# The second gate of an adaLN block held as four columns until the feed-forward, the "+1" of the scale columns moved into the accumulation, and a new order of the work

## The chip, the cores and the metric

The kernel runs on one core of one Trainium2 chip. The metric is the device time of one execution in microseconds (us). Before the change the median of three runs is 200.48 us (200.16 to 200.75). The profiled execution took 200.58 us; its trace spans 198.8 us from the first instruction to the last, and all positions in time below are counted from the start of that span.

## The reference

The block is an adaLN-conditioned transformer layer: a linear attention with learned feature maps, then a gated feed-forward, each behind a layer norm with a scale and a shift that come from a conditioning vector `c`, and each added back through a gate that comes from `c` too.

```python
mod = (_silu(c) @ w_mod).reshape(c.shape[0], 6, 1, -1)
sa, ca, ga, sb, cb, gb = ...                     # six rows of 512
h = _layernorm(x) * (1 + ca) + sa
x = x + ga * _A_ref(h, wqkv, w_phi, wo)          # phi_q, phi_k: softmaxes over 16, twice; linear attention; @ wo
h = _layernorm(x) * (1 + cb) + sb
x = x + gb * _B_ref(h, w_gate, w_up, w_down)     # silu(h @ w_gate) * (h @ w_up) @ w_down
```

`x` is 2048 x 512 in bfloat16, there are 32 heads of 16, and the feed-forward is 1376 wide.

## The kernel before, in words

**Tiles and stages.** The 2048 tokens are 16 tiles of 128, in four chunks of 512. The program runs in three stages that overlap.

The first stage loads `x`, the weights and `w_mod`, forms silu(c) as columns (`silucT`), and folds the feature map into the query and key weights (`fold_phi`, lines 518 to 533). `mod_cols` (lines 463 to 481) forms eight columns of the modulation at a time: 32 TensorE matmuls (line 471) with 128x128 pieces of `w_mod` as weights and one column of `silucT` as data leave four shift columns and four scale columns in one PSUM bank. VectorE copies the shifts (line 476) and copies the scales with 1.0 added (line 477) into `modA` for the first norm and `modB` for the second. `first_norm` and `turn_tile` normalize the first tiles, turn them on TensorE (line 561) and write them, scaled and shifted, as `hT` (ScalarE line 568, VectorE line 570); later tiles are turned by a transposing DMA (`raw`, line 582) and scaled by VectorE, ScalarE or GpSimd (lines 591 to 594).

The second stage takes each tile through `k_tile` (keys on line 625, exponentials on ScalarE line 636, sums on VectorE line 643, values on line 629, products on GpSimd lines 657 to 669), `kv_tile` (accumulation over all tiles into the PSUM tile `kv_ps`, line 675) and `q_tile` (queries line 698, exponentials line 702, sums line 706, the product on GpSimd line 713, and a transposing DMA to `pT`, line 717). `gate(0)` and `gate(1)` (lines 724 to 733) form the two gates here, already spread over all 128 partitions: four 512-column matmuls each, with one column of `silucT` broadcast to 128 as weights (line 730), and a ScalarE copy into `gab` (line 733). GpSimd multiplies the first gate into the output projection (`wo_sb`, line 774).

The third stage takes each tile through `attend` (line 821 on TensorE, lines 824 and 828 on VectorE), a turn, `project` (line 862, then the residual add on line 865 and the statistics of the second norm), the second norm (`xn`, GpSimd line 398 for the first tiles), its turn (`modulate_T`, TensorE line 414, written with `modB` by lines 422 and 425), and the feed-forward (gate and up matmuls on line 920, the narrow last block on line 965, silu on 927, the product on 930 or 936, down matmuls on line 997). The second gate `gab[:, 1]` enters at the very end of a tile, where VectorE multiplies the down result by it (line 1008), and in `wdg` (line 946), half of the down weights with the gate multiplied in, for half of the last tile.

**What sets the order.** Every piece of work is recorded as an operation with its possible engines. A list of numbers, `ORDER` (lines 47 to 87), says in which order they are placed and which alternative each takes (a number's quotient by four is the operation, its remainder the alternative); the class `Plan` places them in that order with assumed durations. Each engine then executes its own operations strictly in the order written, and the SyncE queue issues the DMAs in its own. Six PSUM banks (`one_ps`) are handed out by the same plan. Where the plan expects TensorE to be idle it inserts matmuls of ones on line 1064 (`fill`) whose result is thrown away; there are 26 of them.

## Time and profile before

| | TensorE | VectorE | ScalarE | GpSimd |
|---|---|---|---|---|
| busy, us of 198.8 | 193.6 | 136.2 | 114.1 | 126.5 |

| group of instructions | times | busy, us | mean of one, ns |
|---|---|---|---|
| line 730, a gate: matmul of 512 columns | 8 | 2.1 | 378 |
| line 471, modulation: matmul of 1 column | 64 | 2.0 | 163 |
| line 733, gate copy on ScalarE, 128x512 | 2 | 1.2 | 598 |
| line 774, gate into `wo_sb` on GpSimd, 128x512 | 4 | 4.5 | 1152 |
| line 946, gate into `wdg` on GpSimd, 128x1024 | 2 | 4.2 | 2124 |
| line 713, query product on GpSimd, 128x512 | 16 | 16.8 | 1055 |
| line 476, line 477: copies of four columns on VectorE | 2 and 2 | 0.3 and 0.3 | 157 and 152 |

The duration of one matmul is from its start to its modelled end, and neighbours overlap. What a row of them costs is read from the distance of their starts: four of 512 columns take 0.86 us in the chain of waits, sixteen of one column 0.38 to 0.41 us. In the same way one GpSimd product of 128x512 follows the next after 1.01 to 1.05 us. A busy share near 100% on TensorE counts the filling matmuls too.

### The profile page before, as it was taken

What the parts mean: (1) busy time and instruction counts of PE and PEld (TensorE: products, weight loads), DVE (VectorE), ACT (ScalarE), POOL (GpSimd) and SP (SyncE); (2) the same over time, 40 slices, a digit from 0 to 9 for tenths busy, and PEclk for the clock granted to TensorE, in tenths of its full rate; (3) what the DMA queues carried; (4) which work ended last, traced back from release to release, by engine and by line L of the source; (5) the groups of instructions that cost most, each with busy time, mean ns of one, the idle gap of its engine ahead of it and who ended that gap; (6) DMA issues with size and microseconds to landing.
All of it is one profiled execution on the core that took longest, in us unless ns stands there. A gap on an engine that the chain in (4) does not pass through costs nothing.

```text
span 198.8 us, 4150 instructions
## 1 busy us (share of the span) xinstructions
PE 193.6 (97%) x1529; PEld 115.6 (58%) x1529; DVE 136.2 (69%) x274; ACT 114.1 (57%) x247; POOL 126.5 (64%) x196
## 2 busy tenths in 40 slices
PE   7999999999999999999999999999999999999993
PEld 2755555554565788689766768667444444444442
DVE  5898999999998999999999588452420214340233
ACT  2699999999979975416556544624026510255300
POOL 3377999999999477958956676266725320042841
PEclk9999999999999999999999999999999999999999
DMA  6998997799632883689895543201030000020012
GB/s 210 340 325 191 271 236 239 172 408 244 174 68 53 154 105 74 116 155 148 164 134 104 107 96 66 53 26 43 0 119 0 0 5 26 0 79 0 31 57 76
DMA packets 50983, 24.18 MB, mean 122 GB/s; under 512 B 42161, under 2 KB 47762, under 8 KB 50962
## 3 DMA queue, kind: packets, MB, share of 16 engines
q1 hardware_dynamic: 50816, 23.85, 50.7%
q8 instruction: 12, 0.20, 0.4%
q14 instruction: 9, 0.07, 0.1%
q10 hardware_dynamic: 146, 0.07, 0.1%
HBM read 11.58 MB, written 2.10 MB: 69 GB/s over the span
## 4 chain that ended last, share of the span: by engine, by line
PE 87%; POOL 5%; ACT 4%; DMA 2%; DVE 1%; issue 1%; POOLq 0%; DVEq 0%
PE one_ps L920 35%; PE one_ps L997 19%; PE one_ps L629 7%; PE one_ps L862 6%; PE one_ps L625 5%; PE one_ps L698 3%; PE kv_ps L1064 3%; PE one_ps L965 3%; POOL wo_sb L774 2%; ACT hT L568 2%; PE kv_ps L821 2%; DMA pT<-eq 2%; PE kv_ps L675 2%; ACT e L636 1%; POOL eq L713 1%; PE one_ps L730 1%
## 5 line engine op out<-in xcount | busy, mean ns | idle before, releaser
L920 PE MATMUL one_ps<-hT,wgu_sb 128*128 128x256 bf16 (+2 forms) x560 | 74.7, 288 | 0.0
L920 PEld LDWEIGHTS <-wgu_sb 128*128 128x128 bf16 x560 | 48.3, 98 | 24.0
L927 ACT ACTIVATE sg<-one_ps 128x512 bf16<-128x512 f32 (+1 forms) x41 | 23.7, 587 | 40.4 <-PE one_ps L920 38.9
L936 POOL TENSOR_TENSOR gu<-usb,sg 128x512 bf16<-128x512 bf16 x18 | 20.7, 1153 | 31.4 <-ACT sg L927 25.7
L997 PE MATMUL one_ps<-wd_sb,gu 128*128 128x512 bf16 (+2 forms) x176 | 39.6, 372 | 0.0
L930 DVE TENSOR_TENSOR gu<-one_ps,sg 128x512 bf16<-128x512 f32 (+1 forms) x23 | 15.2, 659 | 29.5 <-PE one_ps L920 22.4
L997 PEld LDWEIGHTS <-gu 128*128 128x128 bf16 (+1 forms) x187 | 18.1, 98 | 18.0
L1008 DVE TENSOR_TENSOR fg<-one_ps,gab 128x512 bf16<-128x512 f32 (+1 forms) x16 | 10.7, 668 | 21.0 <-PE one_ps L997 21.0
L348 DVE BATCH_NORM_STATS2 st<-x_c 128x6 f32<-128x512 bf16 x32 | 21.2, 678 | 0.2
L643 DVE TENSOR_REDUCE S<-e 128x64 f32<-128x1024 bf16 x16 | 19.0, 1200 | 0.4 <-ACT e L636 0.2
L706 DVE TENSOR_REDUCE Sq<-eq 128x64 f32<-128x1024 bf16 x16 | 19.0, 1195 | 0.0
L934 ACT CAST usb<-one_ps 128x512 bf16<-128x512 f32 x18 | 10.5, 586 | 12.9 <-PE one_ps L920 12.8
L702 ACT ACTIVATE eq<-one_ps 128x512 bf16<-128x512 f32 x32 | 17.1, 609 | 0.1
L713 POOL TENSOR_TENSOR eq<-eq,Rq 128x512 bf16<-128x512 bf16 x16 | 16.8, 1055 | 0.5
L636 ACT ACTIVATE e<-one_ps 128x512 bf16<-128x512 f32 x32 | 16.8, 618 | 0.0
L1012 POOL TENSOR_TENSOR ot<-x_c,fg 128x512 bf16<-128x512 bf16 (+1 forms) x10 | 11.0, 1105 | 8.1 <-DMA out_dram<-ot 4.3
L862 PE MATMUL one_ps<-wo_sb,oT 128*128 128x512 bf16 x64 | 15.9, 379 | 0.0
L629 PE MATMUL one_ps<-wv,hT 128*128 128x512 bf16 x64 | 15.6, 379 | 0.2 <-ACT e L636 0.2
L698 PE MATMUL one_ps<-wq,hT 128*128 128x512 bf16 x64 | 15.8, 379 | 0.0
L625 PE MATMUL one_ps<-wk,hT 128*128 128x512 bf16 x64 | 15.7, 379 | 0.0
L398 POOL TENSOR_SCALAR xn<-x_c,ln_mv,ln_nmr 128x512 bf16<-128x512 bf16 x14 | 10.6, 768 | 1.8 <-DVE ln_nmr L384 1.8
L669 POOL TENSOR_TENSOR e<-e,S 128x512 bf16<-128x512 bf16 x11 | 11.5, 1054 | 0.1
(118 smaller groups left out, 276.6 us busy)
## 6 DMA issues: line engine op xcount, KB each, us to landing
wmod_sb<-in_w_mod_dram SPq DMA_DIRECT2D x2, 1024.0 KB, 6.5
out_dram<-ot SPq DMA_DIRECT2D x15, 128.0 KB, 1.9
x_c<-in_A_x_dram SPq DMA_DIRECT2D x3, 512.0 KB, 4.4
wgu_sb<-in_B_w_gate_dram SPq DMA_DIRECT2D x1, 1376.0 KB, 6.4
wgu_sb<-in_B_w_up_dram SPq DMA_DIRECT2D x1, 1376.0 KB, 10.3
wd_sb<-in_B_w_down_dram SPq DMA_DIRECT2D x1, 1280.0 KB, 6.3
wmod_sb<-in_w_mod_dram SPq DMA_DIRECT2D x2, 512.0 KB, 6.1
wk<-in_A_wqkv_dram SPq DMA_DIRECT2D x1, 512.0 KB, 4.8
```

The lines of the kernel that those rows point to most:

```text
L348: pl.op("DVE", r=reads, w=[st6], us=0.6, fn=lambda: nc.vector.bn_stats(st6()[:], src))
L625: nc.tensor.matmul(pk()[:], lhsT=hT[c_i][k][:, cols], rhs=Wk2[:, k, :], start=(k == 0), stop=(k == KD - 1))
L629: nc.tensor.matmul(v()[:], lhsT=hT[c_i][k][:, cols], rhs=wv_sb[:, k, :], start=(k == 0), stop=(k == KD - 1))
L636: nc.scalar.activation(e()[:, :, sg].rearrange("p g h f -> p g (h f)"), pk()[:].rearrange("p (g n) -> p g n", g=G), ACT.Exp, scale=(1.0, - ...
L643: pl.op("DVE", r=[e], w=[Ss], us=1.14, fn=lambda: nc.vector.tensor_reduce(Ss()[:].rearrange("p g s h -> p (g s h)"), e()[:].rearrange("p g ...
L698: nc.tensor.matmul(pq()[:], lhsT=hT[c_i][k][:, cols], rhs=Wq2[:, k, :], start=(k == 0), stop=(k == KD - 1))
L706: pl.op("DVE", r=be, w=[Sq], us=1.14, fn=lambda: nc.vector.tensor_reduce(Sq()[:].rearrange("p g s h -> p (g s h)"), eq[:].rearrange("p g s ...
L862: nc.tensor.matmul(a()[:], lhsT=oT()[:, j0 + j, :], rhs=wo_sb[:, j, :], start=(j == 0), stop=(j == KD - 1))
L920: nc.tensor.matmul(ps_()[0:fsz, q * n:(q + 1) * n], lhsT=wgu_sb[:, k, i, m * P:m * P + fsz], rhs=h2[k], start=(k == 0), stop=(k == KD - 1))
L927: pl.op("ACT", r=[g, btab], w=[sg], us=0.08 + 0.41 * L / CW, fn=lambda: nc.scalar.activation(sg()[0:fsz, 0:L], g()[0:fsz, 0:L], ACT.Silu))
L936: pl.op("POOL", r=[usb, sg], w=[gu], us=0.17 + 0.98 * L / CW, fn=lambda: nc.gpsimd.tensor_tensor(gu()[0:fsz, 0:L], usb()[0:fsz, 0:L], sg() ...
L997: nc.tensor.matmul(fp()[:], lhsT=b()[0:fsz, c0:c0 + P], rhs=wd_[0:fsz, m, wcs], start=(m == 0), stop=(m == FM - 1))
```

## The change

The change has four parts.

1. **Second gate as columns.** `gate(1)` no longer makes 512-column matmuls. Sixteen one-column matmuls (line 751 of the changed file) leave the gate as four columns of 128 in PSUM, and one small copy (line 754, on VectorE) puts them in `gcol`. The first gate stays as it was.
2. **Spread later.** A new `spread_gate`, recorded just before the feed-forward's weights are prepared, writes a matrix with four 128x128 blocks, each the identity times one column of the gate (line 761, recorded for GpSimd or VectorE; the order takes GpSimd), sums it over the partitions with one 512-column matmul whose weights are all ones (line 765), and copies the result to `gab[:, 1]` (line 766, on ScalarE). The end of the preparation now waits for `gcol` in place of the spread gate.
3. **The 1 of the scales in PSUM.** In `mod_cols` one more matmul (line 480: a row of ones against four ones) adds 1 to the four scale columns in the bank, so that one copy of eight columns takes the place of a copy and an add, and may be on VectorE (as for `modA`) or on ScalarE (as for `modB`). The option of reading the scales straight from PSUM for the first tiles is written in but switched off (`early = False`).
4. **A new `ORDER`.** The whole list is different, so the order of instructions on every engine, the order of the DMAs, the engines chosen and the filling matmuls differ too.

Read from the two built programs, with a number for each that the prediction uses: the filling matmuls go from 26 to 24 (two of them in the third stage before, one after). The two halves of the first `w_mod` load had followed each other; now a 256 KB piece of `x` is queued between them. Of the two later 1 MB loads of `w_mod` the one with the second gate comes first. The columns of `modB` are now formed about 2.7 us of matmuls earlier in the TensorE order. All statistics of the third chunk (line 348) now stand before the first key sum on VectorE. Line 761 stands on GpSimd behind the four `wo_sb` products and one query product, and ahead of two query products and the second norm of tile 0; a `wdg` product of 128x512 stands between the second norms of tiles 0 and 1. The two large loads of the gate and up weights (`wgu_sb`) now stand behind two `pT` transposes and the down weights in the DMA queue.

```diff
 ORDER = [
-    0, 4, 44, 8, 48, 64, 52, 12, 16, 68, 76, ...
+    0, 4, 8, 44, 12, 132, 48, 20, 136, 116, 64, ...
...
                 nc.tensor.matmul(mp()[:, n:n + 1], lhsT=wmod_sb[:, k, (n0 + n) * P:(n0 + n + 1) * P],
-                                 rhs=silucT[:, k:k + 1], start=(k == 0 and n == 0), stop=(k == KD - 1),
+                                 rhs=silucT[:, k:k + 1], start=(k == 0 and n == 0), stop=(k == KD - 1 and n < KD),
                                  skip_group_check=True)
+            if k == KD - 1:
+                nc.tensor.matmul(mp()[:, KD:2 * KD], lhsT=ones[0:1, 0:P], rhs=ones[0:1, 0:KD], start=False, stop=True,
+                                 skip_group_check=True)
 
         def fc():
-            nc.vector.tensor_copy(mt[:, 0:KD], mp()[:, 0:KD])
-            nc.vector.tensor_scalar_add(mt[:, KD:2 * KD], mp()[:, KD:2 * KD], 1.0)
+            nc.vector.tensor_copy(mt[:], mp()[:])
...
-        pl.op("DVE", r=[mp], w=[b], us=0.2, fn=fc)
+        pl.op([("DVE", 0.1, fc), ("ACT", 0.2, lambda: nc.scalar.copy(mt[:], mp()[:]))], r=[mp], w=[b])
...
     def gate(gi):
         col0 = (2 * D, 5 * D)[gi]
+        if gi == 0:
...
+            return
+        mp = bank("fold", [P, KD])
+
+        def fm():
+            for k in range(KD):
+                for j in range(KD):
+                    nc.tensor.matmul(mp()[:, j:j + 1], lhsT=wmod_sb[:, k, col0 + j * P:col0 + (j + 1) * P], rhs=silucT[:, k:k + 1],
+                                     start=(k == 0 and j == 0), stop=(k == KD - 1), skip_group_check=True)
+        pl.op("PE", r=[bsil, bm2[gi]], w=[mp], us=0.43, fn=fm)
+        pl.op([("DVE", 0.1, lambda: nc.vector.tensor_copy(gcol[:], mp()[:])),
+               ("ACT", 0.2, lambda: nc.scalar.copy(gcol[:], mp()[:]))], r=[mp], w=[bgcol])
+
+    def spread_gate():
+        bd = Buf()
+
+        def fd(eng):
+            eng.tensor_tensor(gab[:, 1].rearrange("p (j m) -> p j m", j=KD), ident_b[:].unsqueeze(1).to_broadcast([P, KD, P]),
+                              gcol[:].unsqueeze(2).to_broadcast([P, KD, P]), op=ALU.mult)
+        pl.op([("POOL", 1.02, lambda: fd(nc.gpsimd)), ("DVE*", 0.62, lambda: fd(nc.vector))], r=[bgcol], w=[bd])
         t = bank("fold")
...
+        pl.op("PE", r=[bd], w=[t], us=0.216, fn=lambda: nc.tensor.matmul(t()[:], lhsT=ones[:, 0:P], rhs=gab[:, 1], start=True, stop=True))
+        pl.op([("ACT", 0.49, lambda: nc.scalar.copy(gab[:, 1], t()[:])), ("DVE", 0.6, lambda: nc.vector.tensor_copy(gab[:, 1], t()[:]))],
+              r=[t, bd], w=[bgab[1]])
...
-    turned = pl.op("NONE", r=bKVZ + bgab + [bmodB, bmodA] + bWq2, w=[bturn], us=0.0, fn=f_turn)
+    turned = pl.op("NONE", r=bKVZ + [bgab[0], bgcol] + [bmodB, bmodA] + bWq2, w=[bturn], us=0.0, fn=f_turn)
...
+    spread_gate()
     wdg = wts.tile([P, FM, D // 2], BF16, name="wdg")
```

## The prediction

> **What bounds the kernel now.** I read four views in this order: the engine totals, busy time by stage, the chain of waits, and the timelines of TensorE and GpSimd around the place where the chain leaves TensorE. First the busy times of TensorE, its weight loads, VectorE, ScalarE and GpSimd in three stages (clock, DMA share and GB/s at the end of a row):
>
> ```profile
> 20.00:40.00 20.00, 20.00 (x171) 10.55 (x169) 19.41 (x32) 19.84 (x47) 20.00 (x29) 1.00 0.90 232
> 40.00:57.00 17.00, 17.00 (x148) 9.09 (x147) 16.58 (x22) 16.27 (x44) 16.92 (x22) 1.00 0.84 254
> 57.00:68.00 11.00, 10.93 (x105) 6.30 (x104) 10.39 (x26) 9.60 (x24) 8.83 (x14) 1.00 0.36 69
> ```
>
> From 20 to 57 us four engines are full at once, so a saving on one of them alone moves nothing by itself. After 68 us only TensorE is full. The chain that ended last says who leads (start, length, what):
>
> ```profile
> 53.77 0.88 PE one_ps L629 x4
> 54.65 0.26 POOL S L661
> 54.91 0.07 issue
> 54.98 1.06 POOL e L669
> 56.03 3.33 POOL wo_sb L774 x3
> 59.36 0.21 POOL Rq L709
> 59.57 1.11 POOL wo_sb L774
> 60.69 1.01 POOL eq L713
> ...
> 64.41 3.22 DMA pT<-eq
> ...
> 67.68 0.43 PE kv_ps L821 x8
> ```
>
> For ten microseconds the chain is GpSimd, then one transposing DMA; before and after it is TensorE. The two timelines show how close they run (GpSimd's norm of tile 0, then TensorE's turn of it):
>
> ```profile
> 64.37 0.77 POOL L398 TENSOR_SCALAR xn<-x_c,ln_mv,ln_nmr 128x512 bf16<-128x512 bf16 x1
> ```
>
> ```profile
> 65.08 0.42 PE L821 MATMUL kv_ps<-KVZ,pT 128*128 128x68 bf16 x8
> 65.33 0.39 PE L414 MATMUL one_ps<-ident_b,xn 128*128 128x128 bf16 x4
> 65.56 1.03 PE L698 MATMUL one_ps<-wq,hT 128*128 128x512 bf16 x4
> ```
>
> The norm ends at 65.14 and the turn starts at 65.33 without idle time: GpSimd and TensorE meet there with no slack on either side. I call that start T0. Counting matmul columns at 0.2166 us per 512 in the two orders, exactly 127.5 us of matmuls stand behind T0 in both kernels. So the change in time is the shift of T0, plus the waits that TensorE gains or loses behind it. Behind T0 the trace of before has two, 0.15 us in the first gate matmuls and 0.22 us ahead of the fifth attend tile (67.68, waiting for the `pT` of the chain). From there to 194.2 us TensorE runs without a wait.
>
> **What the skill says.** The Trainium skill, "Perfetto Trace Analysis", section Optimization Strategy: a kernel can have several regimes with different most-contended engines, and one looks in the regime for what blocks. The rows above agree: full on four engines, then TensorE alone. "TensorE: Matmul & The Clock Gate", section Back-to-back issue gap, gives about 25 ns as the floor for up to 64 columns and 518 cycles at 2.4 GHz, 216 ns, for 512; the trace has 0.38 to 0.41 us for sixteen one-column matmuls of line 471 and 0.86 us for the four of line 730, so both prices hold here. "DMA: Bandwidth & Descriptors", section Why a DMA increments its semaphore by 16 and not by 1: a transfer counts as landed when the last of its engines is done. The trace agrees: the second 1 MB piece of `w_mod`, issued at 25.91 us, had all but one or two of its packets started by 31 us and landed at 33.10.
>
> **The change, part by part.**
>
> *Second gate.* TensorE loses 0.86 us (line 730) before the attention and gets sixteen one-column matmuls there, 0.40 us (as line 471): -0.46. Later it gets one 512-column matmul, 0.22 us, where a filling one of the same size is dropped, so behind the last key-value product nothing changes. ScalarE's copy of 0.60 us moves from the full stage to about 62 us, where a query exponential waits behind it; the small copy of `gcol`, 0.15 us as on line 476, goes to VectorE. The spread itself is not in the trace. Its nearest row is line 713, a GpSimd product of the same 128x512 with a broadcast operand: 1.055 us each, 1.02 as distance. Bounds are 1.0 and 1.15 (line 774, no broadcast). I take 1.02. It stands on GpSimd behind the four `wo_sb` products and one query product; behind it are two query products, and then the norm that T0 waits for. So it is paid in full on the chain shown above: +1.02.
>
> *The 1 in PSUM.* Two tiny matmuls, 0.05 us on TensorE. A copy and an add of 0.15 us each, overlapping, become one copy: some 0.1 us of VectorE, not on the chain. I cost it at nothing.
>
> *Filling matmuls.* 4.79 us of columns become 4.47. They fill time that TensorE spends waiting anyway: nothing.
>
> *The new order, start.* The second half of the first `w_mod` load now follows 256 KB of `x`. In the trace these landings are 9.37 us for the half and 10.04 for the next 256 KB, so it lands 0.67 later, and `modA` is ready near 11.0 instead of 10.23. ScalarE began writing `hT` at 10.73; now it also has one more pair of lines 377 and 378 first, 0.47 us, so 11.2. Four of line 568 at 0.345 us later the first keys can start: 12.7 instead of 12.18. But ScalarE writes ten of these, not twelve: its key exponentials start at 11.2 + 3.45 = 14.65, before 14.85.
>
> *GpSimd to T0.* In before its first key product (line 661) is at 18.95, and it is then busy without a gap over 0.1 us until `wo_sb` at 55.99: 37.04 us. In after this stretch has no statistics pair (lines 381 and 382, -1.34), one norm less (-0.75), one small copy less (-0.17), one `hT` piece more (+0.52) and one line 709 more (+0.21): 35.5 us. It starts later: VectorE has all the statistics of the third chunk first, so its first sum runs 16.95 to 18.1; ScalarE's reciprocal comes after seven exponentials and copies, 14.65 + 4.22 + 0.47 = 19.35; GpSimd's product starts near 19.7. So `wo_sb` starts at 19.7 + 35.5 = 55.2, 0.8 earlier. From there to the norm before took 64.37 - 55.99 = 8.38; now 8.38 - 0.21 + 1.02 = 9.19. The norm runs 64.4 to 65.15, and T0 by GpSimd is 65.15 + 0.19 = 65.35.
>
> *TensorE to T0.* The last key-value product started at 55.34 and ended at 56.37. Now +0.5 for the late start, -0.46 for the gate, -0.33 for filling between the first keys, -0.3 of a 0.4 us wait at 17.6 us that the other order of values should shed: 54.75. One wait is new. `modB`'s 32 matmuls, at 33.67 in before just behind the landing at 33.10, are now reached at 30.8, and all keys, values and queries are queued behind them. The load is issued behind two transposes that I put 1.4 us earlier, so with the same 7.2 us it lands at 31.65; it may be sooner, since the 512 KB of `wo_sb` no longer follow directly. Wait between 0 and 0.85; I take 0.35. Then 55.1, end 56.0, and T0 by TensorE is 65.33 - 0.4 = 64.95. It waits 0.4 us there for GpSimd. The matmul of ones on line 765 waits for the spread too, done at 55.2 + 4.45 + 1.05 + 1.02 = 61.7; TensorE gets there at 61.8, and behind it are only the projection of tile 1 and queries.
>
> *Behind T0.* The fifth attend tile is reached 1.3 us later in the order, so its `pT` has landed: -0.22. The 128x512 `wdg` product, 1.1 us as half of line 946, stands ahead of the norm of tile 1: done by 69.6, needed at 69.9, so hidden. The weights of line 920 arrive about 57 us, needed at 66. The tail, 194.2 us to the end, has the same last operations.
>
> *Sum.* +0.02 at T0, -0.22 behind it: -0.2, so 200.48 - 0.2 = 200.3.
>
> **The rivals.** *Faster, GpSimd is early.* If GpSimd's stretch before `wo_sb` shrinks by more than worked out, TensorE sets T0. Without the `modB` wait it ends the products at 55.6 and reaches T0 at 64.6: -0.73 - 0.22, 199.5. For it: TensorE had next to no wait in this stage, and every key tile is placed earlier (the last by 1.8 us of matmuls). Against it: GpSimd's 37 us without a gap.
>
> *Slower, `modB` waits.* If the second-gate-first order of the loads brings the other piece where it landed before, 33.10, TensorE stands 2.3 us: products end at 58.0, T0 67.0, +1.65 - 0.22, 201.9. If it lands halfway, at 32.4, the wait is 1.6 and T0 66.3: 201.2. A GpSimd stretch with 0.5 us of gaps adds as much, since the norms of tiles 0 and 1 then both come late. I put this case at 201.3. For it: that landing lagged its packets by 2 us. Against it: the issue is earlier and less is queued behind.
>
> **How the numbers follow.** The meeting at T0 with GpSimd last: 0.44, 200.3. TensorE last: 0.32, 199.5. A new wait: 0.24, 201.3. The range 199.3 to 201.4 leaves out about 0.1 on each side. The spread's bounds (1.0 to 1.15) move the middle case by 0.1. Faster by over 0.3% means below 199.9: nine tenths of the second case and a sixth of the first, 0.36. Slower means above 201.1: most of the third, 0.24. Between: 0.40.
>
> **What would show it.** The chain of waits of after should go through GpSimd lines 761 and 722 into the turn on line 415, with 0.2 to 0.6 us of TensorE idle there; the `wo_sb` products should start near 55.2; the first keys near 12.7; the wait of `modB` under 0.9. No GpSimd wait at T0 means the second case. Over 1 us idle at line 476, or idle at the turn of tile 1, means the third. A new TensorE wait after 75 us would be a cause that I have not seen.

## The result, and the profile after

The changed kernel took 201.57 us (median of six runs, 201.28 to 201.94) against 200.66 us (200.16 to 201.14) for the kernel before on the same chip: a ratio of 1.0048, 95% interval 1.0029 to 1.0066. It is slower by about 0.9 us, and lies 0.17 us above the range that I gave. The ratios here and below leave out single runs that lie more than 1.5% above the fastest of the same kernel; the medians do not. Run again later, instruction for instruction the same, it gave 201.68 us and 1.0031 (1.0011 to 1.0051). The profiled execution took 201.28 us, the shortest of the six; its trace spans 199.5 us, 0.7 more than before.

Busy time by stage, the three windows of the prediction, for the changed kernel (TensorE, its weight loads, VectorE, ScalarE, GpSimd; clock, DMA share and GB/s at the end):

```profile
20.00:40.00 20.00, 19.70 (x181) 10.40 (x179) 20.00 (x30) 19.38 (x49) 20.00 (x28) 1.00 0.71 180
40.00:57.00 17.00, 17.00 (x149) 9.09 (x147) 15.84 (x22) 15.82 (x45) 16.58 (x24) 1.00 0.94 295
57.00:68.00 11.00, 10.88 (x98) 6.08 (x96) 10.22 (x26) 9.78 (x23) 9.65 (x13) 1.00 0.32 64
```

VectorE and GpSimd are less busy than before in the second window (15.84 us against 16.58, and 16.58 against 16.92), and still the third stage starts later. In the first window TensorE is idle for 0.30 us; before it was not. The chain of waits around the same place as in the prediction (start, length, what):

```profile
54.73 0.26 POOL S L670
55.06 1.06 POOL e L678
56.12 0.21 POOL Rq L718
56.34 4.46 POOL wo_sb L808 x4
60.79 1.01 POOL eq L722
61.80 1.01 POOL gab L761
62.85 0.38 PE one_ps L765
...
66.07 0.38 PE one_ps L415 x4
```

The spread (line 761) stands in the chain as forecast, 1.01 us long, but the chain leaves GpSimd at line 765, the matmul of ones, not at the norm of tile 0. The `wo_sb` products start at 56.3, not at 55.2. TensorE's timeline, and GpSimd's norm of tile 0:

```profile
30.39 1.03 PE L707 MATMUL one_ps<-wq,hT 128*128 128x512 bf16 x4
31.64 0.95 PE L476 MATMUL one_ps<-silucT,wmod_sb 128*128 128x1 bf16 x32 [0.23 <-DMA wmod_sb<-in_w_mod_dram]
32.52 0.17 PE L480 MATMUL one_ps<-ones 1*128 1x4 bf16 x1
32.63 0.43 PE L684 MATMUL kv_ps<-va,e 128*128 128x68 bf16 x8
...
62.85 0.38 PE L765 MATMUL one_ps<-gab,ones 128*128 128x512 bf16 x1
...
66.06 0.40 PE L415 MATMUL one_ps<-ident_b,xn 128*128 128x128 bf16 x4
```

```profile
65.22 0.78 POOL L399 TENSOR_SCALAR xn<-x_c,ln_mv,ln_nmr 128x512 bf16<-128x512 bf16 x1
```

The start of tile 0's turn, T0, is at 66.06 in place of 65.33: +0.73. The last matmul starts at 195.86 in place of 195.10: +0.76. So behind T0 nothing is gained or lost in sum, and nearly all of the difference is made before T0. Of the 0.73, 0.38 is a later start (first keys at 12.56 in place of 12.18), and 0.43 lies between the first `wo_sb` product and T0 (9.77 in place of 9.34), where the spread now stands. From the first keys to `wo_sb` it takes 43.73 us, hardly less than the 43.81 of before.

For the experiments I read five positions from each trace: the first keys on TensorE (line 625 before, 634 after), GpSimd's first key product S (line 661, 670), its first `wo_sb` product, T0, and the last matmul. The start of a run depends on when loads land, so the distances matter more than the positions: from the first keys to T0 it was 53.15 us before and 53.50 after.

### The profile page after: what moved, and what is told of

The parts are those of the page before. It is cut to its first block, busy times and chain, and to the rows that moved or that the text cites. A ratio compares the mean times of both kernels' runs of the same rounds, so it can differ in the third digit from the quotient of the medians.

```text
span 199.5 us, 4172 instructions
## 1 busy us (share of the span) xinstructions
PE 193.9 (97%) x1542; PEld 115.4 (58%) x1542; DVE 135.2 (68%) x273; ACT 111.5 (56%) x247; POOL 129.2 (65%) x199
## 4 chain that ended last, share of the span: by engine, by line
PE 63%; POOL 5%; DVE 2%; DMA 2%; ACT 1%; issue 1%; DVEq 0%; POOLq 0%
PE one_ps L954 33%; PE one_ps L1032 19%; PE one_ps L896 5%; PE one_ps L1000 2%; POOL wo_sb L808 2%; DMA oT<-o 2%; PE kv_ps L855 1%; POOL e L678 1%; PE one_ps L707 1%; DVE Sq L715 1%; POOL eq L722 1%; POOL gab L761 1%; DVE o L862 0%; ACT e L645 0%; DVE A L858 0%
## 5 line engine op out<-in xcount | busy, mean ns | idle before, releaser
L954 PE MATMUL one_ps<-hT,wgu_sb 128*128 128x256 bf16 (+2 forms) x560 | 73.9, 288 | 0.0
L1047 POOL TENSOR_TENSOR ot<-x_c,fg 128x512 bf16<-128x512 bf16 x9 | 10.4, 1155 | 13.1 <-DVE fg L1043 13.1
L638 PE MATMUL one_ps<-wv,hT 128*128 128x512 bf16 x64 | 16.1, 379 | 0.0
L399 POOL TENSOR_SCALAR xn<-x_c,ln_mv,ln_nmr 128x512 bf16<-128x512 bf16 x15 | 11.5, 778 | 3.9 <-DVE ln_nmr L385 2.9
L899 DVE TENSOR_TENSOR x_c<-x_c,one_ps 128x512 bf16<-128x512 bf16 x16 | 10.7, 678 | 3.1 <-PE one_ps L896 2.5
```

The lines of the kernel that those rows point to most:

```text
L954: nc.tensor.matmul(ps_()[0:fsz, q * n:(q + 1) * n], lhsT=wgu_sb[:, k, i, m * P:m * P + fsz], rhs=h2[k], start=(k == 0), stop=(k == KD - 1))
```

## The experiments

Each kernel was run with the kernel before on the same chip. The text names the median of each kernel, its ratio to the kernel before and the 95% interval. In all experiments the filling matmuls are written out as a list, so that they do not change when the plan does; in experiments 1, 4, 8, 10 to 12, 17 and 18 the one ahead of line 765 is left out. For these and other reasons the line numbers differ by a few, in experiment 10 by more. ORDER entries are quoted with their neighbours. In the traces of the ninth to the twelfth experiment some matmul records are missing; positions there are those of the first instruction of a group.

The distances, in us, from one profiled run each (the second and third columns are the median of all runs and the time of the profiled one):

| kernel | median | profiled | first keys at | first keys to `wo_sb` | `wo_sb` to T0 | first keys to T0 | T0 to last matmul |
|---|---|---|---|---|---|---|---|
| before | 200.66 | 200.58 | 12.18 | 43.81 | 9.34 | 53.15 | 129.77 |
| changed | 201.57 | 201.28 | 12.56 | 43.73 | 9.77 | 53.50 | 129.80 |
| 1 | 201.66 | 201.83 | 13.07 | 43.38 | 9.25 | 52.63 | 130.65 |
| 2 | 200.92 | 201.07 | 12.71 | 43.56 | 9.76 | 53.32 | 129.57 |
| 3 | 200.93 | 200.72 | 12.07 | 43.69 | 9.77 | 53.46 | 129.74 |
| 4 | 200.71 | 202.90 | 14.38 | 43.31 | 9.34 | 52.65 | 130.45 |
| 5 | 201.18 | 200.87 | 12.27 | 43.89 | 9.48 | 53.37 | 129.77 |
| 6 | 201.72 | 201.72 | 12.29 | 43.90 | 10.22 | 54.12 | 129.86 |
| 7 | 200.98 | 201.04 | 12.28 | 43.91 | 9.34 | 53.25 | 130.03 |
| 8 | 201.38 | 201.38 | 13.16 | 43.64 | 9.34 | 52.98 | 129.80 |
| 9 | 202.02 | 201.99 | 13.54 | 43.71 | 9.76 | 53.47 | 129.56 |
| 10 | 200.77 | 202.62 | 13.95 | 43.97 | 9.35 | 53.32 | 129.85 |
| 11 | 200.64 | 202.67 | 15.24 | 43.06 | 9.18 | 52.24 | 129.78 |
| 12 | 201.29 | 201.96 | 13.86 | 43.26 | 9.29 | 52.55 | 130.08 |
| 13 | 201.27 | 201.38 | 12.21 | 44.38 | 9.33 | 53.71 | 130.02 |
| 14 | 201.41 | 201.04 | 12.64 | 43.81 | 9.34 | 53.15 | 129.77 |
| 15 | 201.68 | 202.05 | 12.56 | 44.74 | 9.77 | 54.51 | 129.56 |
| 16 | 200.89 | 201.11 | 12.91 | 43.38 | 9.77 | 53.15 | 129.63 |
| 17 | 200.79 | 200.89 | 12.76 | 43.27 | 9.35 | 52.62 | 130.07 |
| 18 | 200.48 | 200.66 | 12.51 | 43.47 | 9.13 | 52.60 | 130.13 |

In experiments 4, 10, 11 and 12 the profiled run is the slowest or among the three slowest, so its start says nothing of the median. A later start can also shorten the next distance: in experiment 1 the first keys came 0.51 later than in the changed kernel, but the two 1 MB loads of `w_mod` landed no more than 0.16 later, and TensorE waited less for them.

### 1 and 8: the spread out of GpSimd's chain

```diff
 ORDER
-... 708, 1772, 1768, ...
-... 1904, 1776, 1908, ...
+... 1858, 1772, 1916, ...
```

Entry 1772 is the spread, moved behind the norm of tile 0; 1776 (matmul of ones), 1780 (ScalarE copy) and 1792 (a `wdg` product) follow later, in experiment 8 much later. First experiment:

> The changed kernel with the spread of the second gate (lines 761, 765, 766) moved behind the second norm of tile 0 on GpSimd, its ones matmul behind tile 1's projection and tile 0's turn on TensorE, the wdg product of 128x512 after 88 us, and the one filling matmul ahead of line 765 left out; the other filling matmuls are written out as a list so that they stay as they were. Theory (GpSimd's late norm and the wait for the spread set T0): GpSimd's norm starts 1.05 earlier, near 64.2; the 0.27 wait on line 765 and the 0.15 wait at T0 go, and one 0.22 filling matmul goes: T0 near 65.4, 0.6 earlier than 66.06, the end 0.4 to 0.6 earlier (ratio to before 1.001 to 1.003). Rival (TensorE's own late keys, modB wait and one-row matmuls set T0): T0 earlier by no more than 0.2, the end within 0.2 of the changed kernel (ratio about 1.004).

Measured: 201.66 us, 1.0046 (1.0029 to 1.0063): nothing gained. First keys to T0 took 52.63, 0.87 less than in the changed kernel, so more came forward at T0 than expected; 0.35 of it lies before `wo_sb`, where this run waited 0.19 us for loads of `w_mod` and the changed kernel 0.63. But from T0 to the last matmul it took 130.65 in place of 129.80; 0.22 of this is the matmul of ones, which now stands behind T0. ScalarE's timeline shows one place where it went: the copy to `gab` at 69.11 stood ahead of the copy and the table load that the silu needs,

```profile
69.11 0.63 ACT L765 CAST gab<-one_ps 128x512 bf16<-128x512 f32 x1
69.58 0.65 ACT L967 CAST usb<-one_ps 128x512 bf16<-128x512 f32 x1
70.25 1.28 ACT L697 ACT_TABLE_LOAD   x1
```

and TensorE had a gap of 0.31 us near 72 us, ahead of the matmuls of line 1000 (999 here). The eighth experiment puts copy and product elsewhere:

> The changed kernel with the spread on GpSimd behind the norm of tile 0, as in the first experiment, but the matmul of ones and the ScalarE copy near 80 us, where ScalarE stands idle, and the wdg product after 140 us; there the copy had stood ahead of the silu inputs and the weights of tile 0 on ScalarE, and the product ahead of query products. Theory (that placement gave the gain back): T0 0.5 to 0.7 earlier than in the changed kernel, no wait of 0.3 at the first gate and up matmuls of line 1000, end 0.4 to 0.6 earlier, ratio 1.0015 to 1.003. Rival (the wait for the oT transposes and VectorE near 99 us sets the end, whenever T0 comes): the gain at T0 is gone by 100 us, ratio 1.004 to 1.005.

Measured: 201.38 us, 1.0028 (1.0015 to 1.0042). First keys to T0 took 52.98, 0.52 less than in the changed kernel, and T0 to the last matmul 129.80, as there. T0 itself is at 66.14 only because that run started 0.6 later: its first keys are at 13.16. The gap near 72 us is gone. So taking the spread out of the chain gains half a microsecond in this trace, 0.43 of it behind `wo_sb`, and the copy's placement on ScalarE can lose it again. By the medians 0.2 to 0.3 us of it shows, which the intervals can't tell from nothing.

### 2: one engine for each tile's turn

```diff
-... 224, 236, 36, ...
+... 224, 237, 36, ...
-... 308, 249, 548, ...
+... 308, 248, 548, ...
```

> The changed kernel with both halves of tile 1's turn written to hT by VectorE and both of tile 2's by ScalarE, in place of one half each on both engines; nothing else differs. Theory (two engines that read one PSUM bank wait for each other): VectorE's wait of 1.00 us at 13.3 goes, its first key sum comes 0.4 to 0.6 earlier (near 17.0), GpSimd's first key product near 19.8, the norm of tile 0 and the spread 0.3 to 0.5 earlier; the end 0.3 to 0.45 earlier (ratio to before 1.002 to 1.003). Rival (the wait is for the matmuls of the turn or for a statistic, not for the other engine's half): the gap stays and nothing moves. Second rival: the first sum comes earlier, but the gain is used up by another wait before 55 us, since four engines are full: first product earlier, wo_sb products at 56.3 as before.

Measured: 200.92 us, 1.0011 (1.0000 to 1.0023). VectorE's timeline in the changed kernel:

```profile
14.26 0.59 DVE L579 TENSOR_SCALAR hT<-one_ps,modA 128x128 bf16<-128x128 bf16 x2 [1.00 <-ACT hT L577]
```

and here, where only the fourth tile is still split between two engines:

```profile
13.98 0.60 DVE L578 TENSOR_SCALAR hT<-one_ps,modA 128x128 bf16<-128x128 bf16 x2 [0.56 <-ACT hT L576]
```

The wait follows the split: it went from the third tile to the fourth and became shorter. It is a wait for a semaphore that ScalarE raises when it has read its half. From the first keys to S it takes 7.31 us in place of 7.73. The Trainium skill, "PSUM — Partial Sum Buffer", section PSUM bank collisions raise a hardware error, says that the compiler's scheduler puts any two instructions on different engines in order when they touch the same bank and the same group of 32 partitions, ScalarE against VectorE too; these rows agree, with a wait of 1.00 and of 0.56 us. But the `wo_sb` products start at 56.27, as in the changed kernel: in this trace the second rival holds up to T0. The last matmul is 0.26 earlier, from a wait near 99 us that is absent here. That is less than the 0.65 between the medians, and TensorE still waits 0.30 and 0.31 us for the two loads of `w_mod` in this trace.

### 3 and 5: the one-row matmul

Experiment 3 takes it out of the changed kernel, experiment 5 puts it into the kernel before:

```diff
-            if k == KD - 1:
-                nc.tensor.matmul(mp()[:, KD:2 * KD], lhsT=ones[0:1, 0:P], rhs=ones[0:1, 0:KD], start=False, stop=True,
-                                 skip_group_check=True)
...
-            nc.vector.tensor_copy(mt[:], mp()[:])
+            nc.vector.tensor_copy(mt[:, 0:KD], mp()[:, 0:KD])
+            nc.vector.tensor_scalar_add(mt[:, KD:2 * KD], mp()[:, KD:2 * KD], 1.0)
```

> The changed kernel with part 3 undone: no one-row matmul on line 480, the scale columns copied with 1.0 added by VectorE (modB's pair placed some us later in VectorE's order, so that it does not wait there). Theory (a one-row matmul costs TensorE 0.15 to 0.18 us in place of 0.025): modA is ready 0.1 earlier or the same (one more VectorE instruction), the stretch from the last modB matmul to the next one is 0.15 shorter; since GpSimd sets T0, the end moves by 0.1 to 0.2 only (ratio to before 1.0035 to 1.0045). Rival (the gaps around line 480 are a wait that stays without it): the same gaps stand ahead of the next matmul and TensorE gains 0.05 or less.

> The kernel before with part 3 alone: the one-row matmul behind each set of modulation columns, and one VectorE copy of eight columns in place of a copy and an add. Filling matmuls as in the kernel before. Theory (each one-row matmul holds TensorE 0.15 more than the 0.025 I priced, but modA comes by one copy less and T0 is set by GpSimd): 0 to 0.2 slower, ratio 1.000 to 1.001. Rival (the 0.6 gained by undoing part 3 in the changed kernel is the price of the one-row matmuls in any order): 0.4 to 0.6 slower, ratio 1.002 to 1.003.

Measured: without it in the changed kernel 200.93 us, 1.0015 (1.0005 to 1.0025), more than theory or rival gave. In the trace T0 comes 0.53 earlier, 0.49 of it by an earlier start; from the first keys to T0 it takes 53.46, as in the changed kernel. With it in the kernel before 201.18 us, 1.0026 (1.0014 to 1.0038): between theory and rival by the median, the rival by the ratio. TensorE's timeline of the kernel before, where nothing stands between the 32 matmuls and the next keys:

```profile
33.50 0.94 PE L471 MATMUL one_ps<-silucT,wmod_sb 128*128 128x1 bf16 x32
34.31 0.59 PE L625 MATMUL one_ps<-wk,hT 128*128 128x512 bf16 x2
```

From the first of the 32 to the next work it takes 0.81 us here and 0.99 in the changed kernel (31.64 to 32.63, shown above): one one-row matmul costs 0.18. It comes with a gap of 0.07 ahead of it and one of 0.08 behind it, the same in each trace that has it, and both are gone without it. In experiment 5 T0 is 0.31 later (65.64): 0.09 at the first keys, 0.22 after them. The Trainium skill, "TensorEngine Tiling (Array Packing)", section Key Properties, says that changing the tiling mode drains TensorE; a matmul of one row among such of 128 may be such a change; no run here shows whether it is, or changes the mode alone.

### 4, 11 and 12: the edits together

Experiment 4 joins 1, 2 and 3 and places the matmuls of `modB` later; 11 is the same with the placements of experiment 8; 12 has the exchanged loads of experiment 9 as well.

> The three edits together, and the modB matmuls placed behind one more key-value product, one query and one key tile, so that they do not wait for their load. Theory (T0 is late by GpSimd's 0.86 and TensorE's 0.31 together, and each alone hides behind the other): T0 near 64.8, 1.2 earlier than in the changed kernel; the end 0.8 to 1.1 earlier, ratio to before 0.999 to 1.001. Rival (the new order loses its time in the stage of four full engines, whatever the four causes): T0 no earlier than with the late spread alone, 65.4, ratio 1.002 or more.

> The four edits of the fourth experiment together, with the matmul of ones and the ScalarE copy near 80 us and the wdg product after 140 us as in the eighth. Theory: what the fourth lost at 73 and 99 us stays gained, end 0.2 to 0.5 before that of the fourth, ratio to before 0.998 to 1.000. Rival (its end is set by the late landing at the start): as the fourth, 1.0003.

> The same with the two loads exchanged as in the ninth experiment. Theory: another 0.3 to 0.6 earlier, ratio 0.9955 to 0.998, the fastest of all here. Rival: no more than 0.1 earlier than without the exchange.

Measured: 200.71 us, 1.0003 (0.9990 to 1.0017); 200.64 us, 0.9992 (0.9979 to 1.0005); 201.29 us, 1.0032 (1.0020 to 1.0044). From the first keys to T0 it takes 52.65, 52.24 and 52.55 us, 0.8 to 1.3 less than in the changed kernel. The medians of 4 and 11 are 0.86 and 0.93 below its median, so there about as much of it is kept. The profiled runs of 4 and 11 took 2.2 and 2.0 us more than their medians, mainly because they started late, with first keys at 14.38 and 15.24: the second half of the first `w_mod` load landed at 11.84 and 11.17 in place of 9.96, and in 11 TensorE's granted clock was 0.50 from 9.7 to 13.1 us, where the other profiles have 1.00. The single times of 11 go from 199.50 to 204.01. The exchanged loads of 12 gave nothing; it is 0.65 slower than 11.

### 6, 7 and 13: the second gate as columns, in the old order

```diff
-... 708, 1712, ...
+... 708, 1772, 1712, ...
```

Here the kernel before gets parts 1 and 2 of the change, with `gate` and `spread_gate` as in the changed kernel. In experiment 6 the spread stands where the changed kernel has it; in 7 it stands behind the norm of tile 0; in 13 one `hT` piece goes from GpSimd to ScalarE besides (entry 1254 becomes 1253) and two filling matmuls are left out.

> The kernel before with parts 1 and 2 alone: second gate as columns, formed where it was formed, and its spread on GpSimd behind the four wo_sb products and one query product, as in the changed kernel, ahead of the norm of tile 0; matmul of ones and ScalarE copy near 63.5. Filling matmuls as before. Theory (the spread is paid in full on the chain GpSimd - norm - T0): norm of tile 0 1.0 later, near 65.4, T0 near 66.35, end 0.7 to 1.0 later, ratio 1.0035 to 1.005. Rival (0.46 of TensorE and 0.6 of ScalarE saved in the stage of four full engines come back on GpSimd too): T0 within 0.5 of before, ratio below 1.0025.

> The kernel before with parts 1 and 2 alone, but the spread on GpSimd behind the norm of tile 0, where GpSimd stood idle from 65.4 to 67.3, the matmul of ones and the ScalarE copy near 79, where ScalarE stands idle. Theory (what is saved on TensorE before T0 hides behind GpSimd, and the matmul of ones is added behind T0): T0 as before, end 0.0 to 0.25 later, ratio 1.000 to 1.001. Rival (the relief of TensorE and ScalarE in the full stage brings GpSimd forward): T0 0.2 to 0.45 earlier, ratio 0.998 to 0.9995.

> The seventh experiment (kernel before, second gate as columns, spread late) with one hT piece of 128x512 moved from GpSimd (0.73 us at 40.6) to ScalarE, whose gate copy at 44.9 is gone, and without the two filling matmuls ahead of the projection near 60 us. Theory (GpSimd hides what TensorE saves): wo_sb products near 55.5, T0 0.3 to 0.5 earlier than before, end 0.1 to 0.4 earlier, ratio 0.998 to 0.9995. Rival (ScalarE is as full: the keys of that chunk or the exponentials come late): TensorE waits near 44 us, T0 no earlier, ratio 1.000 or more.

Measured: 201.72 us, 1.0048 (1.0036 to 1.0060); 200.98 us, 1.0012 (1.0003 to 1.0022); 201.27 us, 1.0030 (1.0018 to 1.0042). GpSimd's timeline of experiment 6,

```profile
61.87 1.03 POOL L752 TENSOR_TENSOR gab<-ident_b,gcol 128x512 bf16<-128x512 bf16 x1
...
65.58 0.77 POOL L398 TENSOR_SCALAR xn<-x_c,ln_mv,ln_nmr 128x512 bf16<-128x512 bf16 x1
```

and TensorE's, standing idle for the norm at T0:

```profile
66.41 0.40 PE L414 MATMUL one_ps<-ident_b,xn 128*128 128x128 bf16 x4 [0.49 <-POOL xn L398]
```

T0 is 1.08 later than before, and from the first keys to T0 it takes 54.12, +0.97. With the spread behind the norm this is 53.25, +0.10, so 0.87 goes with the place of the spread, most of its 1.03 us. The 0.46 us of TensorE and 0.60 of ScalarE that the columns save bring nothing forward: `wo_sb` starts at 56.19 in both. Experiment 13 asked whether they would if GpSimd had 0.73 less to do. They don't: from the first keys to T0 it takes 53.71. TensorE and GpSimd then wait for ScalarE (TensorE's row, then GpSimd's):

```profile
44.76 1.04 PE L625 MATMUL one_ps<-wk,hT 128*128 128x512 bf16 x4 [0.82 <-ACT hT L592]
```

```profile
45.21 0.25 POOL L661 TENSOR_TENSOR S<-S,R 128x32 f32<-128x32 f32 x1 [1.29 <-ACT R L648]
```

ScalarE is as full as GpSimd, and a 0.7 us piece on it stands ahead of the next chunk's keys.

### 9 and 14: the exchange of two loads at the start

```diff
-    0, 4, 8, 44, 12, 132, 48, 20, 136, 116, 64, 120, 16, 52, ...
+    0, 4, 8, 44, 12, 132, 48, 16, 20, 136, 116, 64, 120, 52, ...
```

Experiment 9 puts the half of `w_mod` (16) ahead of the piece of `x` (20) in the changed kernel; 14 does the opposite in the kernel before.

> The changed kernel with one pair of DMAs exchanged: the second half of the first w_mod load follows the first half directly, as in the kernel before, and the 256 KB piece of x comes after it. Nothing else differs. In the profiles of the changed order so far TensorE waits for this half (it landed between 9.6 and 11.8 us and the matmuls of modA followed each time at once), in the order of before it landed at 9.06 to 9.37 and nothing waited. Theory (the start of the changed kernel is as late as this landing): the half lands near 9.3, modA and the first keys 0.5 earlier than in the changed kernel's own profile, the end 0.3 to 0.6 earlier, ratio 1.002 to 1.0035. Rival (the x piece, now landing 0.6 later, becomes the wait; or GpSimd's first sum does not follow): first key product within 0.2 of 20.3, ratio above 1.004.

> The kernel before with one pair of DMAs exchanged: the 256 KB piece of x ahead of the second half of the first w_mod load, as in the changed order. Nothing else differs. Theory (this exchange is what the new order's start costs): the half lands near 9.9 in place of 9.37, TensorE waits for it at 9.4, modA and the first keys 0.5 to 0.7 later, T0 0.4 to 0.6 later, ratio 1.002 to 1.003, and the single times scatter more. Rival (the late start is made up before T0, since GpSimd's chain has its own pace): first keys late, T0 within 0.2, ratio below 1.001.

Measured: 202.02 us, 1.0066 (1.0044 to 1.0088), slower still; and 201.41 us, 1.0038 (1.0023 to 1.0052). In the kernel before the exchange is a plain shift: the half lands at 9.82, the first keys and T0 come 0.46 later, from one to the other it takes 53.15 as before. In the changed kernel the half did land at 9.29, but VectorE's timeline shows what it met:

```profile
9.96 1.29 DVE L348 BATCH_NORM_STATS2 st<-x_c 128x6 f32<-128x512 bf16 x2 [1.51 <-DMA x_c<-in_A_x_dram]
...
11.97 0.15 DVE L483 COPY modA<-one_ps 128x8 f32<-128x8 f32 x1
```

The statistics of that piece of `x` stand ahead of the copy to `modA` on VectorE; with the piece later, `modA` is ready at 12.1 and not at 10.9. The late start belongs to the new order: load order and VectorE's order fit each other, and moving this one load did not help.

### 10: the new order alone

Parts 1 to 3 undone (second gate by four 512-column matmuls, no spread, copy and add), the list kept:

```diff
-... 708, 1772, 1768, ...
+... 708, 1768, ...
-... 765, 949, 829, ...
```

> The new order alone: the changed kernel's list with parts 1 to 3 undone (second gate spread by four 512-column matmuls and a ScalarE copy, at the place of the columns; no spread later; scales copied with 1.0 added). Filling matmuls as in the changed kernel, less the one ahead of line 765. Theory (the effects add: parts 1 and 2 on the chain +0.96, part 3 +0.4 to 0.5, the sum of all +0.96, so the order gave about 0.45 back): 0.3 to 0.6 faster than before, ratio 0.997 to 0.9985. Rival (the order is what loses time, by its late start and its shared banks, and the spread would hide in it): 0.2 or more slower than before, ratio above 1.001.

Measured: 200.77 us (single times from 200.0 to 202.6), 1.0004 (0.9988 to 1.0020). It neither gains nor loses by what can be told. By the medians the effects do not add: parts 1 and 2 in the old order cost 0.91 us, part 3 there 0.37, the order alone 0.20, and all together 0.91. The intervals are too wide to be sure of it.

### 15 and 16: the wait for `modB`'s load

The changed kernel once more, and the changed kernel with `modB`'s 32 matmuls some 2 us later on TensorE:

```diff
-... 664, 932, 812, ...
+... 1168, 932, 936, 940, 944, 984, ...
```

> The changed kernel itself, instruction for instruction, with its filling matmuls written out as a list as in all edits of it. Theory (the edits overlap: each hides behind the next limit): ratio 1.0045 to 1.005 again, and the second half of the first w_mod load lands within 0.3 of 9.96. Rival (the first six runs lie high, by the landing of that half): ratio 1.002 to 1.0035, and single times that scatter by 1 us and more.

> The changed kernel with modB's 32 matmuls (and the one-row matmul and the ScalarE copy behind them) placed one key-value product, one query and one key tile later on TensorE, about 2 us; nothing else differs. Theory (the wait for their load is passed on in full to T0 and to the end, though GpSimd seemed to set T0): no wait ahead of these matmuls, wo_sb products 0.3 to 0.5 earlier than 56.3, T0 0.3 to 0.5 earlier than 66.06, the end 0.4 to 0.8 earlier than the changed kernel (ratio to before 1.000 to 1.002), and the single times scatter less. Rival (GpSimd's chain sets T0, the wait hides behind it): T0 within 0.1 of 66.06 at the same start, ratio as the changed kernel's, 1.003 to 1.005.

Measured: 201.68 us, single times from 200.80 to 202.59; and 200.89 us, 1.0002 (0.9988 to 1.0015), single times from 200.48 to 201.31. TensorE's timeline of the changed kernel in the second profile, which started like the first (first keys 12.56, S 20.29):

```profile
30.53 1.03 PE L706 MATMUL one_ps<-wq,hT 128*128 128x512 bf16 x4
32.64 0.95 PE L475 MATMUL one_ps<-silucT,wmod_sb 128*128 128x1 bf16 x32 [1.09 <-DMA wmod_sb<-in_w_mod_dram]
...
67.07 0.40 PE L414 MATMUL one_ps<-ident_b,xn 128*128 128x128 bf16 x4
```

The load landed at 32.60, in the first profile at 31.60, with the same issue within 0.2 us. Thirteen of its 512 packets of 2 KB started after 31 us, the last at 31.98; in the first profile the last started at 30.94. Gaps are read from the distance of starts: the four matmuls of queries take 0.86 us, and the 32 came 2.11 us behind the first of them in place of 1.25, so TensorE's gap was 1.25 us in place of 0.39 (the brackets count from the modelled end of the queries). Ahead of the second gate's columns near 25 us, which wait for the other 1 MB piece, it was 0.39 in place of 0.24: 1.01 more together. `wo_sb` started 1.01 later and T0 1.01 later: all of this addition went through. With the matmuls later there is no wait:

```profile
33.33 0.94 PE L475 MATMUL one_ps<-silucT,wmod_sb 128*128 128x1 bf16 x32
...
62.84 0.38 PE L764 MATMUL one_ps<-gab,ones 128*128 128x512 bf16 x1 [0.32 <-POOL gab L760]
```

Here T0 is at 66.06 as in the first profile, with first keys that came 0.35 later: from these to T0 it takes 53.15 us, as before the change. So of the 0.63 us that TensorE waited for the two loads in the first profile 0.35 had gone through. The scatter is halved, and by the medians the loss is gone but for what can't be told. What is left in this trace is the spread, for which TensorE stands idle at 62.8.

### 17 and 18: the spread out of the chain as well, and no one-row matmul

These are experiment 16 with the edits of 8, and of 8 and 3.

> The changed kernel with modB's matmuls later (as in the run before) and the spread out of GpSimd's chain (as in the eighth). Theory (with the load's wait gone, the spread sets T0): no wait ahead of the ones matmul or the projection of tile 1, T0 0.4 to 0.7 earlier than with modB later alone at the same start, ratio to before 0.997 to 0.999. Rival (TensorE's products are the limit and the norm's lateness only fills its waits): T0 0.2 earlier or less, ratio 0.9995 or more.

> The same, and part 3 undone. Theory (two one-row matmuls cost TensorE 0.31 and TensorE now sets T0): another 0.2 to 0.35 earlier, ratio 0.9955 to 0.9975. Rival (GpSimd and ScalarE are as full, so that 0.31 of TensorE is lost in the stage of four full engines): no more than 0.1 earlier.

Measured: 200.79 us, 1.0009 (0.9984 to 1.0034), and 200.48 us, 0.9992 (0.9978 to 1.0006). First keys to T0: 52.62 and 52.60. At T0 the spread is worth 0.53 here, as in experiment 8, and now GpSimd has time to spare:

```profile
64.55 0.77 POOL L398 TENSOR_SCALAR xn<-x_c,ln_mv,ln_nmr 128x512 bf16<-128x512 bf16 x1 [0.56 <-PE one_ps L706]
```

Taking out the one-row matmuls brings the first keys 0.25 earlier and nothing between keys and T0. Most of what comes forward at T0 is lost later: from T0 to the last matmul it takes 130.07 and 130.13 in place of the 129.63 of experiment 16. 0.22 of this is the matmul of ones, now behind T0, and near 98 us stands a gap of 0.27 on TensorE that the first profile of the changed kernel has too. By the medians the step from experiment 16 to 17 can't be told from nothing. VectorE's timeline of that profile shows its likely origin, a buffer that a transposing DMA still reads:

```profile
95.28 0.69 DVE L862 TENSOR_TENSOR o<-kv_ps,A 128x512 bf16<-128x512 f32 x1 [0.80 <-DMA oT<-o]
```

The last kernel has the lowest median of all, a microsecond below the changed kernel (200.48 against 201.57 and 201.68). It can't be told from the kernel before: the interval holds 1.

## Why the prediction was wrong

I forecast 0.2 us faster and got 0.9 slower. T0 was put at 65.35; it was at 66.06, and at 67.07 in the second profile of the same kernel. The start and the way from `wo_sb` to T0 came out no worse than forecast (12.56 for 12.7, and 9.77 for 10.15). What failed lies between: from the first keys to `wo_sb` I expected 42.5 us (55.2 less 12.7), 1.3 less than before, and it took 43.73 and 44.74. The edits of experiment 11 together bring it to 43.06, and of the 0.56 left there 0.5 lies before GpSimd's first product.

**The step that failed most: "Wait between 0 and 0.85; I take 0.35".** I worked out the landing of the second 1 MB of `w_mod` as 31.65 from one trace, and it was 31.60 in the profile; the gap was 0.39. But I made a single number of a time that varies. The next profile had the landing at 32.60 and the gap at 1.25. I had seen the sign of it, and misread it: in the trace of before not one or two but seven of the 512 packets started after 31 us, the last at 32.08, so the load landed late because its last packets were late (by the section that I cited from "DMA: Bandwidth & Descriptors" in the Trainium skill, it counts as landed only when all its engines are done). I had put this into the rival with the chance of 0.24. Placing these matmuls later took 0.7 to 0.8 us off the median. So the third case, "slower, `modB` waits", was the nearest, and the chances were the wrong way round; by its own sign, over 1 us idle at line 476, only the second profile is a case of it. That its time of 201.3 was close is in part luck, since its sum held nothing for the late first product below. I also let the wait end in TensorE's column, to be hidden by GpSimd, but 0.35 of the first profile's 0.63 reached T0 (experiment 16), and all of the 1.01 that the second had more: keys, exponentials, sums and GpSimd's products all stood behind it in turn. The wait of 0.24 for the second gate's columns, the other load of the pair, I had not seen at all.

**"So `wo_sb` starts at 19.7 + 35.5."** The 35.5 was right: where TensorE waits 0.2 us or less for the two loads, GpSimd takes 35.5 to 35.7 us from its first product to `wo_sb` (experiments 1, 11, 12, 16, 17, 18). The 19.7 was not: it was 20.29 with the first keys 0.14 earlier than forecast. VectorE's first sum was at 17.50 in place of 16.95, because of a wait of 1.00 us for ScalarE's half of the same tile's turn. I had counted ScalarE's ten pieces and VectorE's six and not asked whether the two may read the tile at once. Removing it for one tile brought S 0.42 forward against the first keys, but `wo_sb` only 0.17 (experiment 2). And with the `modB` wait the 35.5 did not set `wo_sb` at all: 20.29 + 35.5 = 55.8, while it started at 56.29 and 57.30.

**"Two tiny matmuls, 0.05 us on TensorE".** They cost 0.18 each at their place, 0.31 at T0 in the kernel before. I had priced them by the issue floor of a one-column matmul in a row of its like. In the changed order nothing of the second reaches T0 (experiments 3 and 18: from the first keys to T0 as without the edit), so the term was mis-sized by some 0.2.

**"So it is paid in full on the chain shown above: +1.02."** Right in kind, and nearly in size where it was taken from: 1.03 us as duration, 0.87 by its place in the old order (experiments 6 and 7), 0.52 and 0.53 in the new one (experiments 8 and 17), where TensorE is the next limit. The saving of 0.46 on TensorE was rightly not carried to T0.

**"TensorE gets there at 61.8", no wait at line 765.** Not right. The spread ended at 62.80, TensorE waited 0.27 and the matmul started at 62.85; at the turn itself it waited 0.15, where I expected 0.4. This follows from the late `wo_sb`, and the wait is in front of everything on TensorE, so from there GpSimd's lateness reached T0 by two ways.

**The start.** First keys forecast at 12.7, found at 12.56; the landing forecast 0.67 later, found 0.59 later. The exchange alone costs 0.46 us at T0 and 0.74 by the median in the kernel before; a shift of 0.5 at the first keys was in my numbers, and is right.

**Behind T0: -0.22.** The sum was +0.03. The two waits of before are gone, 0.37, but TensorE waits 0.16 at the projection near 72 us and 0.25 near 99 us. I had named a new wait after 75 us as a cause that I had not seen. The columns behind T0 add up to 128.8 us, not 127.5, but they are the same in both traces, so nothing hangs on it.

**What stays open.** The gains of experiments 2 and 3 by the medians, 0.65 each, are larger than their traces show from the first keys to the last matmul (0.41 and 0.10), and with that of experiment 16 they add to more than the edits give together. Both leave the waits for the loads in place, so the medians alone do not single out the wait for `modB`; what does is that the same kernel, with 1.01 more of these waits, had T0 1.01 later. The second half of the first `w_mod` load landed between 9.6 and 11.8 us in the profiles of the new load order and between 9.06 and 9.60 in those of the old one; a profile catches one run, and only its own landings are known. Why the first half, queued behind the same loads in both, also landed anywhere from 7.1 to 9.9 was not tried.

## What to carry to other kernels

When matmuls are placed just behind the landing of their own load, forecast the wait as a range with the landing's scatter, not as the value of one trace, and ask what stands behind it: in a stage where all engines were full, between a half and all of a wait of TensorE went through to the others (experiments 15 and 16). In such a stage work taken from TensorE and ScalarE was worth nothing (experiment 7), and that relief of the other engines would free it is not shown; work added to the engine that the next stage waits for was paid for the most part, so look for an idle stretch of that engine first. A list that orders several engines has its load order built in: here a late start could not be mended by moving one DMA.

## What the runs showed of the hardware

- A matmul with one row of weights and four columns cost TensorE 0.18 us among matmuls of 128 rows, gaps of 0.07 and 0.08 us around it included, where a one-column matmul of 128 rows takes 0.025.
- VectorE waited 1.00 us to read its half of a PSUM tile until ScalarE had read the other half, and ScalarE 0.31 us the other way round; the program's semaphores hold them apart. Where one engine read all of the tile the wait was gone.
- A 1 MB load issued at 24.95 and 25.11 us landed at 31.60 and 32.60 in two runs of the same program, with the same loads in front of it; the last of its 512 packets of 2 KB started at 30.94 and 31.98.
